# Another order of 1589 words for block-sparse attention and a token and channel mixer on one Trainium2 core

## The chip, the cores and the metric

The kernel runs on one core of one Trainium2 chip. The core has five engines that run side by side, each through its own instructions in a fixed order: TensorE (PE in the profile, with PEld for its weight loads), VectorE (DVE), ScalarE (ACT), GpSimd (POOL) and SyncE (SP). They meet at semaphores. Transfers are done by 16 DMA engines, which POOL, SP and ACT give work to. The metric is the device time of one execution in microseconds (us), lower is better. The time before is 292.2 us, the median of three runs (292.03 to 292.49).

## The reference

Attention over 4 batches, 8 heads, 768 positions and 64 features, with a mask in blocks of 32; then, on the 512 features of the joined heads, a mixer over tokens and one over channels.

```python
scores = scale * np.matmul(q, k.transpose(0, 1, 3, 2))
mask = np.abs(blk_i - blk_j) <= 1                   # neighbours
mask |= (blk_i == 0) | (blk_j == 0) | (blk_i == 23) | (blk_j == 23)
# ... and three sampled key blocks for each query block
scores = np.where(mask, scores, -1e9)
x = softmax(scores) @ v                             # heads side by side: [4, 768, 512]
a1 = alpha1 * x + beta1
u = x + lam * np.einsum('ts,bsd->btd', w_tok, a1)   # token mixer, 768 x 768
a2 = alpha2 * u + beta2
out = u + lam * (np.maximum(a2 @ w_ch1, 0.0) @ w_ch2)   # hidden layer of 2048
```

## The kernel before

**Words.** All work is cut into steps of a fraction of a microsecond up to a microsecond, and a step is called by a word: letters for the kind, a number for the piece, and after a colon a PSUM bank or the engine that copies (d: VectorE, a: ScalarE). A string named ORDER lists 1589 words. The kernel goes through it once and emits each word's instructions; a last pass ties the instructions of each engine to that order. Nothing else schedules. Two words on the same engine run in ORDER's order; words on different engines run as soon as the semaphores let them.

```python
    for word in ORDER.split():
        ...
        step[kind](int(n), *args)
    bank_order(tc, list(nc.cur_bb.bb.instructions), psum[:].tensor.name, 8)
    pin_order(nc, tc)
```

**Attention.** The 32 heads are 16 pairs. A pair's scores are cut into nine units of 1024 columns, numbered through: pair p has units 9p to 9p+8.

- lq, lk, lv load a pair's queries, keys and values (L437, issued by POOL, converted to 16 bits on the way, six buffers in turn). A load waits for its buffer and for the landing of the load eight before it. F and a tiny copy on POOL (L435) hold later loads back until DVE gets to F.
- cq, ck, cv put what was loaded into the layout that is needed (L419 on ACT, L421 on DVE).
- For the pairs 0 to 4, H transposes one head on PE (L355), and hq, hk copy queries and keys out of PSUM (L419, L421). The mask of blocks rides along as 24 more rows of queries and keys, so these matmuls have 88 rows. hm copies the 24 rows for the second head's query buffer (L587). For the pairs 5 to 15, tq and tk transpose by DMA, issued by SP (L593).
- q computes a unit's scores into two PSUM banks. q0 to q44 are matmuls of 88 rows (L624). From q45 on, a q word is four matmuls of 64 rows by 256 columns (L634), two of which run side by side in the halves of the array.
- e is the exp of a unit on ACT, 1024 columns from PSUM to SBUF (L645).
- m masks a unit of the pairs 5 to 15 on DVE by a minimum with a table (L655). The table is made once: M writes 24 rows (L532, DVE) from the mask rows in the fourth query buffer, which a transfer on SP (L401) fills ahead of ORDER; N spreads them to DRAM and O reads them back (L538 and L545, SP).
- p and r multiply by the values (L661), n and nt divide by the sums into x (L709, L712, L695, L696).

**Token mixer.** lt loads w_tok in three parts (L460), lt1 for W2 and W3, lt2 for W4 and W5, lt0 for W0 and W1. W transposes one block on PE (L496) and w copies it (DVE). lc loads alpha, beta and lam; L scales them (L506, L508). a and b make the mixer's input (L733, L739), k is 18 matmuls (L763), and x adds the result to x (L772).

**Channel mixer.** lw and lx load its weights (L479, L485), S, T, P and V prepare them. u casts x, U transposes it (on PE at L806 or by DMA at L800). The first batch's hidden layer is f, four matmuls of 384 columns into one bank (L828), emptied by g with bias and relu on ACT (L842) or DVE (L844); it is the stretch f0 to f31, and f32 to f63 are half of the next batch. Later hidden layers use fewer products: y is two matmuls (L997), d and D finish them (L1023, L1025, L866, L1033, L1035), after sums of weights and inputs by V and Y. The second layer is h, eight matmuls of 256 columns (L907), with sums A before and o after it on DVE (L866). s stores (L934). z is a filler matmul on zeros (L315), which keeps PE busy near the start.

**Banks.** PSUM has eight banks. A PE word that writes a bank waits until ACT or DVE has read what stood in it. A q word takes two banks; f, k, h, y, H and W take one.

The order at the start, before ORDER, is fixed: first loads, mask rows, the first head's transposes. The first q word starts at 5.83 us.

Of the kernel before, what the change touches and what calls it, by code (L numbers as in the profile page):

```python
# [72 lines left out]
m58 e59 p46 h17 m53 u8:a m47 u9:a q57:2 q55:3 F36 o2 e57 p47 U4 o14 p51:3 m59 h4 ck11:a m56 p52 e55
p53 nt15 lk14 q63:2 nt17 h18 e63 o3 q64:1 m57 q54:3 e64 q71:2 m60 h5 o15 e54 p57:2 a5 p58 h6 e71 b5
p59 ck12:a m64 q70:2 q62:3 nt19 e70 h19 lk10 m71 e62 q69:1 m54 q61:2 h20 F47 A5 ck9:a m55 p54:6
cq9:a k11:7 lv11 o16 e61 o4 tq9 lq13 h7:1 x11 cq10:a m62 k10:0 tk9 e69 m61 lv9 p60:7 A6 q67:2 tq10
m69 p55 e67 p56 o6 q80:1 x10 p61 e80 p62 nt18 q66:2 h8 nt20 e66 m70 q78:1 ck10:a q68:3 a6 p69:0 e68
p70 lk13 h9 m66 b6 e78 p71 o7 q65:2 q76:3 m63 u10:a q75:1 e65 nt23 h10 m67 u11:a p63:0 cv8:d k12:4
e76 m65 U5 lq12 m68 p66:5 e75 p64 x12 p67 tk10 p68 o8 q81:3 nt22 q86:1 e81 p65 h11 nt21 e86 m75
q74:2 q73:3 a7 e74 k13:0 b7 e73 q72:1 x13 q77:2 o9 u12:a k14:0 u13:a m76 e72 U6 k15:6 x14 A7 e77  # L80
p75:0 p76 x15 q79:1 u14:a m72 q85:2 u15:a h12 m77 e79 U7 m73 p77 e85 q82:3 m80 q93:1 s5 h13 m78 e93
tq11 m79 p78:4 p72:5 m74 e82 p73 p79 tk11 o10 p80 p74 q84:1 P1:d q87:3 nt24 e84 s0 f37:1 m86 tk12
f35:5 e87 nt26 f39:2 ck13:d g35:a m84 lq14 f54:3 g37:a nt25 g39:a q89:2 cv9:d q95:3 e89 q94:0 g54:d
lv10 f38:2 m82 e95 f32:3 P5:d P7:d f34:4 g32:a P6:d f48:5 e94 ck14:d m85 lk15 p84:3 a8 g34:a q83:3
q98:0 e83 p85 cq12:d f47:4 F44 F41 cv11:d tq12 lv15 m81 e98 p86 f61:6 g47:d lv12 g48:a p81:7 m83
q92:0 g61:a q88:2 b8 g38:a p82 f49:6 nt28 e92 m98 f36:2 e88 g49:d f63:3 m89 g36:a q106:0 m87 q91:2
g63:a p83 f51:6 e106 nt27 f56:2 m88 g51:a p87:3 cq13:d e91 f41:7 V0 m94 p88 g56:a q90:0 q96:2 cv10:d
g41:a m93 f52:2 e90 m92 p89 f57:6 m95 g52:a f53:7 e96 V2 p93:2 nt29 g57:a q97:0 q99:2 cq14:d e97
f33:3 m96 tq14 m91 p94 e99 p95 k16:6 m97 tk13 g33:a nt31 g53:a q104:0 m90 q102:1 s2 e104 q103:2 x16
f62:7 s1 a9 e102 tq13 p90:6 p91 p96:0 m99 p92 g62:a p97 nt30 tk14 p98 e103 f60:1 nt32 q113:1 m104  # L90
g60:a q100:2 s3 q105:3 e113 m102 s4 f59:0 b9 k17:1 e100 m113 F45 m103 lq15 e105 f55:2 x17 f44:3 lv14
g59:a m100 g55:a q108:2 m106 q107:0 lv13 e108 q101:3 m105 k18:2 a10 e107 p102:4 f50:5 m108 e101 x18
p99:0 p100 b10 g50:a f58:1 m101 g44:a p103 g58:a q131:3 m107 q115:1 p105:5 A20 e115 f45:1 A12 p106
e131 p104 A16 p101 p107 nt33 g45:a q112:1 k21:6 nt34 e112 nt35 q116:0 A21 q111:1 e116 q130:2 a11
# [5 lines left out]
p129:6 u19:a p130 m128 p131 e117 U9 k23:7 a12 e132 h40 o26 U10 nt43 cv15:a h41 x23 b12 u23:a q138:1  # L100
m127 q118:2 q119:3 e118 o34 h32 V5 cv13:a h21:0 m132 e119 m134 k25:4 o27 e138 k24:5 A14 x25 q142:1
o18 q143:3 A15 p126:4 p127 e143 x24 h33 m118 e142 p132:5 m117 h34 m138 p133 o28 p134 q141:1 nt44
q139:3 e141 p117:1 m143 p128 p118 h22 e139 nt42 m119 q135:1 a14 q125:2 e135 k22:6 b14 u24:a p119
e125 x22 h23 m141 u22:a q120:1 nt39 q140:2 e120 q137:3 U11 m142 k29:1 o19 e140 V1 k28:2 m125 u25:a
x29 e137 p141:3 U12 p142 m120 p143 h24 u29:a m139 m140 q123:2 q121:3 o20 e123 p138:1 x28 p139 h25
# [973 lines left out]
```

## Time and profile before

| | |
|---|---|
| median of three runs | 292.2 us (292.03 to 292.49) |
| the profiled execution | 291.82 us, of which the span from first to last instruction is 290.1 us |
| granted TensorE clock | 1.000 |
| exps on ACT, L645 | 145 instructions, 140.4 us |
| q matmuls, L634 and L624 | 396, 29.8 us, and 120, 25.8 us |
| h matmuls, L907 | 672, three groups of 35.8, 24.6 and 24.4 us |
| f matmuls, L828 | 256, 45.9 us |
| k matmuls, L763 | 576, 36.8 us |
| masks on DVE, L655 | 99, 61.2 us |
| moved by DMA | 30.95 MB, mean 107 GB/s |

The view of groups lists busy time per line, engine and operation. Busy time adds instructions that overlap on an engine once; a matmul's end is modelled, so the starts of matmuls are the surer numbers. A view of windows gives each engine's busy time in a stretch; a view of waits says which engine stood still before which line and what it waited for last; the chain is the series of steps that ended last; the timeline lists instructions in order, merging like ones. Idle time in square brackets stands ahead of an instruction.

### The profile page before, as it was taken

What the parts mean: (1) busy time and instruction counts of PE and PEld (TensorE: products, weight loads), DVE (VectorE), ACT (ScalarE), POOL (GpSimd) and SP (SyncE); (2) the same over time, 40 slices, a digit from 0 to 9 for tenths busy, and PEclk for the clock granted to TensorE, in tenths of its full rate; (3) what the DMA queues carried; (4) which work ended last, traced back from release to release, by engine and by line L of the source; (5) the groups of instructions that cost most, each with busy time, mean ns of one, the idle gap of its engine ahead of it and who ended that gap; (6) DMA issues with size and microseconds to landing.
All of it is one profiled execution on the core that took longest, in us unless ns stands there. A gap on an engine that the chain in (4) does not pass through costs nothing.

```text
span 290.1 us, 8529 instructions
## 1 busy us (share of the span) xinstructions
PE 283.9 (98%) x3538; PEld 213.6 (74%) x3538; DVE 263.8 (91%) x595; ACT 234.0 (81%) x350; POOL 53.3 (18%) x102
## 2 busy tenths in 40 slices
PE   8899999999999999999999999999999999999995
PEld 3677888755677878866677877888766788866884
DVE  5689997689999999999999999999999998699983
ACT  5999998849999999999999999968989860279500
POOL 8545734300621241024005000000000000000000
PEclk9999999999999999999999999999999999999999
DMA  6999999999983498499278002404110140330014
GB/s 161 189 246 210 195 211 194 203 165 176 168 115 30 53 140 118 74 164 135 27 186 146 7 2 57 85 3 47 37 75 0 19 112 0 148 145 1 2 42 177
DMA packets 47927, 30.95 MB, mean 107 GB/s; under 512 B 28792, under 2 KB 43984, under 8 KB 47888
## 3 DMA queue, kind: packets, MB, share of 16 engines
q0 software_dynamic: 15936, 15.21, 34.6%
q1 hardware_dynamic: 31340, 14.32, 24.3%
q10 hardware_dynamic: 612, 0.87, 0.8%
q8 instruction: 28, 0.46, 0.6%
q14 instruction: 11, 0.09, 0.1%
HBM read 31.16 MB, written 6.88 MB: 131 GB/s over the span
## 4 chain that ended last, share of the span: by engine, by line
PE 87%; ACT 5%; DMA 4%; DVE 2%; issue 1%; POOL 0%; ACTq 0%
PE psum L907 26%; PE psum L997 13%; PE psum L828 12%; PE psum L661 11%; PE psum L763 11%; PE psum L634 9%; PE psum L624 4%; DMA wtk<-in_moe_w_tok_dram 3%; ACT hts L842 2%; ACT eT L645 2%; DMA k2f<-in_k_dram 1%; PE psum L806 1%; PE psum L355 1%; DVE a1p L733 0%; ACT rel L419 0%
## 5 line engine op out<-in xcount | busy, mean ns | idle before, releaser
L645 ACT ACTIVATE eT<-psum 128x1024 f16<-128x1024 f32 (+1 forms) x145 | 140.4, 1028 | 9.3 <-PE psum L634 5.4
L655 DVE TENSOR_TENSOR eT<-eT,maskT 128x960 f16<-128x960 f16 x99 | 61.2, 650 | 0.0
L907 PEld LDWEIGHTS <-hts 128*128 128x128 bf16 x480 | 45.1, 98 | 8.5 <-issue 2.1
L661 PEld LDWEIGHTS <-eT 128*128 128x128 f16 x1152 | 44.4, 97 | 8.3 <-issue 1.7
L661 PE MATMUL psum<-vext,eT 128*128 128x65 f16 x1152 | 48.5, 193 | 0.0
L828 PE MATMUL psum<-uT,w1b 128*128 128x384 bf16 (+1 forms) x256 | 45.9, 327 | 0.1
L1023 ACT ACTIVATE snap<-psum,b1t 128x384 f32<-128x384 f32 x44 | 23.7, 581 | 17.7 <-PE psum L997 13.4
L763 PE MATMUL psum<-a1p,wtokT 128*128 128x128 bf16 x576 | 36.8, 219 | 0.2 <-DVE x_sb L772 0.2
L763 PEld LDWEIGHTS <-wtokT 128*128 128x128 bf16 x576 | 33.2, 98 | 4.1 <-DVE x_sb L772 0.8
L907 PE MATMUL psum<-w2t,hts 128*128 128x256 bf16 x288 | 35.8, 273 | 0.0
L866 DVE TENSOR_TENSOR x_sb<-x_sb,psum 128x256 f32<-128x256 f32 (+1 forms) x61 | 30.7, 514 | 4.7 <-PE psum L907 4.5
L828 PEld LDWEIGHTS <-w1b 128*128 128x128 bf16 x256 | 23.0, 98 | 16.1 <-ACT b1t L419 0.9
L842 ACT ACTIVATE hts<-psum,b1t 128x384 bf16<-128x384 f32 x53 | 29.2, 602 | 0.9 <-PE psum L828 0.5
L634 PE MATMUL psum<-qx,kx 64*128 64x256 bf16 x396 | 29.8, 272 | 0.0
L866 DVE TENSOR_TENSOR hts<-snap,psum 128x384 bf16<-128x384 f32 x48 | 24.7, 547 | 2.7 <-PE psum L997 2.3
L624 PE MATMUL psum<-qx,kx 88*128 88x512 bf16 (+1 forms) x120 | 25.8, 326 | 1.3 <-ACT eT L645 1.0
L907 PE MATMUL psum<-w2b,ss 128*128 128x256 bf16 x192 | 24.6, 273 | 0.0
L907 PE MATMUL psum<-w2b,hts 128*128 128x256 bf16 x192 | 24.4, 273 | 0.0
L634 PEld LDWEIGHTS <-kx 64*128 64x128 bf16 x396 | 15.2, 94 | 8.4 <-issue 3.5
L907 PEld LDWEIGHTS <-ss 128*128 128x128 bf16 x192 | 18.0, 98 | 3.8 <-issue 0.6
L772 DVE TENSOR_TENSOR x_sb<-x_sb,psum 128x384 f32<-128x384 f32 x32 | 17.4, 546 | 1.0 <-PE psum L763 0.8
L997 PEld LDWEIGHTS <-w1b 128*128 128x128 bf16 x128 | 12.1, 98 | 6.6 <-DVE hts L866 0.3
(103 smaller groups left out, 362.5 us busy)
## 6 DMA issues: line engine op xcount, KB each, us to landing
out_dram<-x_sb SPq DMA_DIRECT2D x17, 256.0 KB, 2.6
v<-in_v_dram POOLq DMA_DIRECT2D x16, 192.0 KB, 6.3
k<-in_k_dram POOLq DMA_DIRECT2D x15, 192.0 KB, 6.2
q<-in_q_dram POOLq DMA_DIRECT2D x15, 192.0 KB, 7.1
...
```

The lines of the kernel that those rows point to most:

```text
L624: nc.tensor.matmul(t[:, f : f + w], kx[h][0:KC, ts(jt, P)], qx[h][0:KC, c : c + w], start=True, stop=True,)
L634: nc.tensor.matmul(t[:, (2 * a + j) * TH : (2 * a + j + 1) * TH], kx[h][r, ts(2 * g + j, P)], qx[h][r, ts(th, TH)], start=True, stop=True,)
L645: nc.scalar.activation(eTs[n][:, c], t[:, c], AF.Exp, bias=EXPB, scale=SCALE)
L655: nc.vector.tensor_tensor(out=e, in0=e, in1=mask, op=ALU.min)
L661: nc.tensor.matmul(ops[key][:, t * VW : t * VW + D + 1], eTs[n][:, c : c + P], vext[n // NU % NV][:, a, jt, 0 : D + 1], start=(first and z ...
L763: nc.tensor.matmul(t[:, j, :], wtokT[:, s, ts(3 * g + j, P)], a1p[p][:, s, :], start=(s == 0), stop=(s == NT - 1),)
L828: nc.tensor.matmul(hps[i][:, 0:w], w1b[:, dk, ts(f, P)], uT[b][:, dk, hf * HS : hf * HS + w], start=(dk == 0), stop=(dk == 3),)
L842: nc.scalar.activation(hts[kk][:, f, :], t[:, 0:HS], AF.Relu, bias=b1t[:, f : f + 1], scale=1.0)
L866: nc.vector.tensor_tensor(out=out, in0=in0, in1=in1, op=op)
L907: nc.tensor.matmul(cps[b, q][:, side * HD : (side + 1) * HD], lhs[:, nk, :], rhs[:, nk, :], start=(z in (0, 6) and nk == 0), stop=(nk == H ...
L997: nc.tensor.matmul(chains[key], lhs[:, dk, ts(f, P)], rhs[:, dk, :], start=(z in (0, 1, 5) and dk == 0), stop=(dk == 1), skip_group_check= ...
L1023: nc.scalar.activation(dst, t, act, bias=bias, scale=1.0)
```

## The change

Only ORDER differs. Both strings have the same 1589 words if the part behind the colon is left aside: every load, matmul, exp, copy and store is done once in each. What differs is the order, the bank that a PE word uses, and in 58 words the engine. On ACT the casts cq4, cq5, cq7, cq15, cv5, cv7, cv8 and further u, g, d and D words come from DVE, and ck5, ck7, ck12, cv12 and others go to DVE; in sum cq on ACT goes from 3 to 7, ck from 8 to 5, cv from 4 to 6, g from 53 to 51 and D from 28 to 31. The words named in the change's title: M, which writes the rows of the mask's table, is called behind the 18th exp instead of the 41st; lq3 is the thirteenth load word instead of the eighth; tq6 keeps its place on SP, behind tq7 and ahead of tk8, tk7 and tq8, but the cast that it needs, cq6, moves from among the exps before the first hidden layer to near the end of that layer. The last words of ORDER, from h82 on, are the same in both.

The diff, cut to the stretches that the prediction speaks of:

```diff
--- before
+++ after
@@ the first 29 us @@
-lv0 lk1 lq1 q0:0 lt1 q3:1 cq0 e0 lq2 q2:2 H1:6 lk2 e2 hq1:d q1:0 lv1 z480:7 hm0 z480:7 e1 hk1:d
-cv0:d q5:2 ck1:d e3 lq3 q4:0 p0:6 lt0 e4 p1 p2 lt2 q6:1 cq1:d e5 p3 lk3 p4 H2:7 H3:0 lc2 e6 hk2:d
-q7:2 lc0 F35 W2:1 hq2:d e7 lc1 q8:1 hq3:d r4:7 lk4 r5 w2:d e8 q9:2 cq2:d r6 F24 ck2:d lv2 r7 e9 n0
-z480:1 q12:1 lq6 hk3:d r8 e12 q11:2 n1 W3:6 q10:0 e11 w3:d H5:7 cv1:d q16:1 hk5:d e10 lq4 H4:6 hk4:d
-W1:4 e16 q15:0 hq5:d p9:5 e15 p10 hq4:d q13:1 F21 cq3:d W0:7 F46 w1:d e13 lv4 q14:0 p11 W5:4 e14
-ck3:d q25:1 F22 w0:d lk5 p12 w5:d e25 p13 q19:3 n2 W4:4 e19 H6:0 F28 lx3 w4:d q22:1 hk6:d r13:1
-q17:2 e22 L1 q20:3 hq6:d e17 q24:1 L0 r14 H7:0 e20 q18:2 ck4:d a0 lv3 r15 e18 r16 r17 lc5 b0 q23:3
-e24 cv2:d k1:4 n3 lk6 e23 lx1 q21:1 cq4:d r22:1 F42 x1 H9:5 e21 lv6 q28:3 F38 a1 p18:4 lw0 e28 r23
+lv0 lq1 lk1 lt1 lk2 q0:0 q1:1 lq2 cq0 e0 q3:2 F22 hm0 lt2 H1:6 e3 lt0 hq1:d q2:0 lc0 z480:7 F24
+hk1:d e1 lv1 cv0:d q4:2 q6:3 e2 lc1 cq1:d q5:1 lc2 e4 p0:0 lq3 p1 ck1:d e6 lv2 q7:2 z480:1 lk3 p2
+e5 H2:1 q8:3 hk2:d e7 p3 p4 hq2:d H3:2 W2:3 e8 n0 q9:2 W3:1 hq3:d e9 r4:0 q10:3 F42 ck2:d r5 hk3:d
+lk4 r6 e10 q11:2 w3:d lw0 r7 F26 cq2:d r8 e11 w2:d q14:3 lv3 F23 n1 H5:1 e14 q13:1 lc5 hk5:d H4:4
+z480:0 e13 hk4:d q15:3 W4:0 hq4:d e15 W5:5 hq5:d q12:1 W0:4 w4:d e12 q17:3 w0:d q16:0 w5:d e17
+W1:4 cv1:d q23:1 w1:d lq4 p9:5 e16 p10 M0 r13:4 p11 lc4 L1 r14 e23 q18:3 F34 L0 lw1 p12 r15 e18 a0
+q26:0 r16 r17 e26 b0 q25:1 n3 q19:3 p13 q22:0 F21 e19 cq3:d F28 n2 k0:4 lk7 e22 ck3:d q20:3 lq8 x0
...
@@ M0 before @@
-u1:a M0 p36:0 v1:a F39 u5:d p37 p38 x6 q41:1 u6:d U0:1 e41 q43:2 u7:d U2:6 S6 p39 e43 U3:7 v0:d
...
@@ first hidden layer, f0 to f31 @@
-q44:1 v2:a v3:d p40 q42:2 F26 S7 r40:1 r41 e44 f0:6 f6:7 e42 f3:2 g0:a f5:3 cq5:d g3:d f1:6 tq5 lq11
-g5:a F31 n8 r42 f8:2 N0 r43 g8:d f17:0 tk5 f24:3 r44 g24:d f9:2 tk6 S1 f11:3 g9:a g1:d f15:4 ck7:a
-S4 f25:2 g11:a n9 f19:5 F30 S3 f12:1 S2 f2:3 g12:a S0 f31:6 g19:a S5 g15:a f26:1 T0 g2:a f10:4 f4:3
-g10:a T1 f28:5 g26:a f20:4 g31:a T2 g25:a f16:1 ck8:a f7:2 a4 g4:a f23:6 g17:a T3 O0 f13:3 g7:a tq7
-g28:a f18:0 cq8:d cv5:d g13:a f22:5 cv7:d tq6 g16:d g6:a f21:2 g23:d g22:a f27:1 g18:a tk8 P3:d
-g20:a g21:d f14:3 g27:a P2:d f29:2 tk7 g14:a F34 b4 lk11 f30:0 g29:d lk9 tq8 cq11:d q53:2 g30:a
+r42 e44 r43 cq8:d p37 S6 f9:3 lv5 cq5:a F27 S1 p38 q39:0 g9:a tq5 lq9 f0:4 e39 f5:3 N0 f6:6 g5:d
+f14:7 tk5 S4 f22:3 p39 tk6 p40 f7:0 n8 f11:1 g7:a F43 S0 r44 g11:a S3 f1:2 S5 f17:0 g1:a S2 f30:1
+g6:a T0 f16:2 g22:a f8:6 g17:a g14:d cq7:a f27:3 ck8:a f10:0 g27:d f3:7 F37 T1 g10:a f23:3 g0:a
+g3:d f15:0 T2 f13:4 g15:a f2:7 g16:a cv6:d f20:0 T3 g13:a f4:2 g2:a O0 n9 tq7 cv5:a f26:4 F38
+f12:7 a4 g26:a f19:5 g4:a b4 f18:4 F32 g12:d g19:a f21:2 F31 g8:a g30:d g20:d g23:a f29:5 cq6:a
+f28:1 g29:d cq9:a f25:0 tq6 F30 P2:d lq10 g18:d f24:3 g28:a P1:d g25:a lv8 f31:4 tk8 P3:d g21:a
+g24:d lk10 q51:0 g31:a h14:5 P4:d tk7 e51 lk11 A0 q49:1 q52:3 A8 lq13 e49 h0:4 tq8 A4 lk9 e52 o12
...
```

More of the change, by code (lines that the diff above doesn't have):

```diff
@@ L73 @@
[L73 to L94, printed above, removed]
@@ L100 @@
[L100 to L105, printed above, removed]
@@ new lines @@
+g24:d lk10 q51:0 g31:a h14:5 P4:d tk7 e51 lk11 A0 q49:1 q52:3 A8 lq13 e49 h0:4 tq8 A4 lk9 e52 o12
+q48:0 q50:1 A9 h15 e50 A1 o0 q47:3 P0:a A2 k8:2 A10 e47 h1 A5 e48 x8 h2 m49 A11 q45:0 q46:1 e45
+q53:3 m51 h16 tq9 m48 e53 p51:0 m52 k9:1 e46 o1 m53 p52 u8:a x9 q60:3 q58:1 m50 e60 p48:1 p49 m46
+p50 e58 h3 o13 F33 nt16 u9:a q59:3 m45 q57:1 e59 h17 A3 m47 e57 q56:3 p45:1 o14 p53 m58 e56 h18
+m57 ck10:a q54:1 o2 q55:3 nt17 h4 e54 lv9 o15 p57:0 e55 m59 p58 p46 o3 p47 cq10:a q61:1 m54 q63:3
+p59 e63 h5 lv7 nt15 nt19 e61 q70:3 a5 q68:0 h6 e70 b5 p54:2 m56 e68 k11:3 m55 ck9:a m61 q71:0
@@ new lines @@
+q62:3 m60 e71 p55 tk9 lq11 p56 x11 h19 e62 nt18 tq10 o4 q65:0 q66:1 e65 q75:3 m62 k10:4 U4 m70 e75
+m63 h7:0 ck11:a m71 tk10 p60:1 x10 h20 e66 lk13 A6 p61 cv8:a o6 q69:1 o16 q64:3 e69 h8 lk12 F45
+m65 m68 e64 p62 h9 nt20 cv7:a m69 q67:1 q78:2 m66 e67 q73:3 lq14 p69:1 m64 p70 p71 e73 p66:2 o7
+p63:3 m67 h10 e78 a6 p64 u11:a q76:3 nt23 q86:2 u10:a p65 b6 e86 p67 U5 p68 nt21 k13:1 e76 nt22 o8
+q80:1 x13 q72:2 q79:3 e72 A7 h11 a7 u13:a k12:1 e80 b7 m78 q85:2 e79 k15:2 x12 m80 u12:a k14:1 e85
+o9 U6 x15 q77:3 x14 q84:2 u15:a q74:1 m75 u14:a p78:1 h12 e77 m79 U7 m73 p79 e74 q82:3 m72 h13 m76
@@ new lines @@
+p89 f58:4 e90 nt29 f50:6 cv11:d a9 g56:a lv15 f37:5 g53:a m91 k16:7 g58:a g37:a m94 g50:a m90
+q102:0 q97:1 e102 q100:2 b9 k17:6 F46 cq12:d x16 e97 tq12 lk15 f39:0 e100 m97 p93:1 p94 p95 x17
+g39:a q106:1 m100 q98:2 e106 q105:3 tq14 k19:0 m92 e98 cv12:d m102 p90:2 tk13 f47:3 x19 e105 nt31
+p96:4 p91 g47:a s1 p97 m98 p92 u16:a f42:5 s0 m106 u17:a tq13 p98 nt30 g42:a q101:0 q107:3 nt32
+e101 q99:1 k18:5 tk14 V4 e99 a10 f63:4 s4 e107 m105 f59:0 s5 x18 s2 f32:1 g63:a m107 s3 g59:a
+f41:5 V0 g32:a q103:1 m99 g41:a q104:3 q111:0 e103 A20 p105:4 f33:5 b10 e111 p106 m103 p107 f35:2
@@ new lines @@
+A12 e104 k21:3 nt35 g33:a m104 g35:a q110:0 x21 q113:2 q112:3 m101 p102:2 e112 k20:3 A16 A21 e113
+p103 p104 x20 p99:6 e110 f43:7 nt34 A17 p100 g43:a p101 q108:0 m111 q109:1 f46:7 m110 e109 m113
+h35:4 e108 nt33 h28:5 o30 g46:a A22 q134:0 o24 q115:1 e134 q129:3 a11 h36 u21:a m109 f40:0 e129
+m108 h37 m134 e115 b11 p108:1 p109 u19:a m129 f44:6 u20:a A18 h29 g40:a m115 cq15:a f45:0 V2
+ck15:a p110 o31 h30 V5 u18:a tk15 g45:a nt36 h38 g44:a o25 U10 m112 q116:0 q130:1 A23 e116 q114:3
+h31 o32 tq15 e114 m116 p111:0 p112 o26 k23:1 cv14:a U9 m114 cv13:a V1 p113 p114:6 nt37 p115 e130
@@ new lines @@
+p116 h39 nt38 x23 q131:1 q118:3 o33 e131 q126:0 h32 a12 s11 e118 U8 h40 m130 e126 o27 q133:1
+q139:3 A19 e133 h41 m131 h33 e139 m126 o34 q128:0 q127:1 b12 e128 q117:3 A13 h34 m133 u23:a p129:4
+e117 o28 p130 p131 h21:0 nt43 e127 m118 q132:2 q119:3 m127 e132 q138:1 k22:1 m139 e138 m132 p126:4
+k25:5 m128 e119 x22 p127 o18 u22:a q120:1 x25 q140:3 e120 U11 p132:1 m117 p128 h22 A14 e140 A15
+p133 p134 cv15:a m119 q141:1 q125:3 e141 m138 k24:5 nt44 e125 h23 nt42 x24 p138:1 o19 q124:1
+q123:2 a14 e124 q142:3 p139 h24 Y8 e123 m140 p117:2 p118 o20 u24:a p119 b14 p140 e142 h25 nt39
```

78 lines of the change are left out of this document (40 added, 38 removed).

## The prediction

> **What bounds the kernel now.** I read the page first, then busy time by stage, then the list of PE's own waits, then the chain and the timelines at the places these named.
>
> ```profile
> span 290.1 us, 8529 instructions
> ...
> PE 283.9 (98%) x3538; PEld 213.6 (74%) x3538; DVE 263.8 (91%) x595; ACT 234.0 (81%) x350; POOL 53.3 (18%) x102
> ...
> PE 87%; ACT 5%; DMA 4%; DVE 2%; issue 1%; POOL 0%; ACTq 0%
> ```
>
> PE is busy for 98% of the span and carries 87% of the chain. No word is added or dropped, so the same matmuls run. The change can win only time in which PE stands still and what PE pays for the order itself; it can lose wherever a reordered word comes too late. The stages show where PE stands still now:
>
> ```profile
> core 0: us, PE busy (x) PEld busy (x) DVE busy (x) ACT busy (x) POOL busy (x), PEclk, DMA share, GB/s
> ...
> 5.80:12.00 6.20, 5.38 (x67) 3.56 (x68) 3.75 (x10) 5.47 (x7) 4.19 (x8) 1.00 1.13 175
> 12.00:20.00 8.00, 7.62 (x104) 5.45 (x102) 6.99 (x18) 7.89 (x9) 4.10 (x7) 1.00 1.20 208
> 20.00:29.00 9.00, 8.82 (x134) 6.53 (x132) 8.41 (x22) 8.91 (x11) 4.59 (x7) 1.00 1.23 238
> 29.00:50.00 21.00, 21.00 (x368) 17.88 (x365) 18.82 (x54) 20.22 (x24) 11.03 (x20) 1.00 1.16 200
> ...
> 62.00:76.00 14.00, 13.89 (x86) 7.55 (x85) 13.27 (x24) 12.06 (x32) 1.00 (x2) 1.00 1.21 186
> ...
> 120.00:206.00 86.00, 86.00 (x1265) 65.68 (x1261) 84.29 (x184) 79.80 (x109) 8.67 (x15) 1.00 0.46 77
> 206.00:286.90 80.90, 80.90 (x719) 61.85 (x716) 73.14 (x158) 46.44 (x95) 0.00 (x0) 1.00 0.18 62
> ```
>
> From 5.8 to 29 us PE lacks 0.82 + 0.38 + 0.18 = 1.38 us, and ACT is busy 7.89 of 8.00 and 8.91 of 9.00: there the exps on ScalarE set the pace. After 120 us PE has no gap at all. PE's waits by name:
>
> ```profile
> PE psum L624 <- ACT eT L645: 1.0, 2, 0.8
> ...
> PE psum L496 <- DMA wtk<-in_moe_w_tok_dram: 0.4, 2, 0.2
> ...
> PE psum L763 <- DVE x_sb L772: 0.2, 1, 0.2
> ```
>
> So the ground to be won lies in the first 29 us, a little in the first hidden layer (62 to 76 us), and in one token-mixing step.
>
> **The changes of array shape.** From pair 5 on, a q word is four matmuls of 64 rows (L634), and all other words use 128 rows.
>
> ```profile
> 87.61 0.54 PE psum L634 x8
> 88.15 0.98 PE psum L907 x8
> 89.13 0.49 PE psum L661 x16
> 89.62 0.87 PE psum L907 x8
> ...
> 94.30 0.76 PE psum L634 x12
> ```
>
> Twelve q matmuls take 0.76 and eight 0.54, so four cost 0.22 and a run has 0.10 on top. The h word ahead of a q run takes 0.98 where another takes 0.87: 0.11 more. A run of q words thus pays 0.21 us, however long it is. Counted in the two orders, the 99 such words stand in 46 runs before and in 44 after: 2 x 0.21 = **-0.4 us**. No wait is involved, so nothing can hide or undo it.
>
> **The first 29 us: the second head's keys.** DVE copies the second head's queries (hq1), then the mask rows (hm0, L587), then the keys (hk1), and PE's next q word needs the keys.
>
> ```profile
> 7.81 0.55 DVE L421 COPY qx<-psum 64x768 bf16<-64x768 bf16 x1 [0.81 <-PE psum L355]
> 8.38 0.35 DVE L587 COPY qx<-qx 24x768 bf16<-24x768 bf16 x1
> 8.74 0.56 DVE L421 COPY kx<-psum 64x768 bf16<-64x768 bf16 x1
> ...
> 9.40 1.02 PE L624 MATMUL psum<-qx,kx 88*128 88x256 bf16 x5 [0.79 <-ACT eT L645]
> ```
>
> The wait at 9.40 is named after ACT, but the keys were finished at 9.30. After, hm0 stands ahead of hq1 and fits into DVE's 0.81 us of idleness; hk1 follows hq1 at once. PE goes on at about 9.05: -0.35 us.
>
> **The first 29 us: the mixing weights.** W words transpose wtk, which arrives in three loads.
>
> ```profile
> 5.28 0.57 POOL L460 DMA_DIRECT2D wtk<-in_moe_w_tok_dram  x1
> ...
> 10.70 1.11 POOL L460 DMA_DIRECT2D wtk<-in_moe_w_tok_dram  x2
> ...
> DMA to landing us min/median/max: 8.0/8.3/9.5
> ```
>
> ```profile
> 12.47 0.60 PE L624 MATMUL psum<-qx,kx 88*128 88x512 bf16 x2
> 13.28 0.54 PE L496 MATMUL psum<-identb,wtk 128*128 128x128 bf16 x6 [0.22 <-DMA wtk<-in_moe_w_tok_dram]
> ...
> 18.45 0.50 PE L355 MATMUL psum<-identb,rel 128*128 128x128 bf16 x6
> 19.10 0.51 PE L496 MATMUL psum<-identb,wtk 128*128 128x128 bf16 x6 [0.15 <-DMA wtk<-in_moe_w_tok_dram]
> ...
> 23.07 0.60 PE L624 MATMUL psum<-qx,kx 88*128 88x512 bf16 x2
> 23.50 0.50 PE L496 MATMUL psum<-identb,wtk 128*128 128x128 bf16 x6
> 23.84 0.50 PE L355 MATMUL psum<-identb,rel 128*128 128x128 bf16 x6
> ```
>
> Undisturbed, a q word takes 0.43 (23.07 to 23.50) and a W or H word 0.34 (23.50 to 23.84). So W2 at 13.28 lost 13.28 - 12.47 - 0.43 = 0.38, and W1 at 19.10 lost 19.10 - 18.45 - 0.34 = 0.31. (The view shows less, 0.22 and 0.15, because a matmul's modelled end hides some 0.16 of each wait.) Both started as their load landed: 5.28 + 8.0 = 13.28. After, lt1 is still the fourth load and lands at 13.3 again. Ahead of W2 now stand, from 9.05 on, five q words (2.15), five p (0.245 each, from the 0.49 for 16: 1.2), two H (0.7) and a filler (0.2): 13.3, no wait to speak of. lt2 moves from tenth to seventh in the load queue, and lt0 from ninth to eighth with the same bytes ahead of it, so it lands at about 19.0 as before; but the words that use it, W0 and W1, now stand behind W4 and W5, which use lt2. From W2 to W4 PE has six q (2.6), four W or H (1.4), four and a half r (1.1) and a filler (0.2): 18.6; W0 comes 1.1 us later, 0.7 after its load. Both waits go: -0.7 us. The cover is thin for W2; without it 0.38 comes back.
>
> The page "DMA: Bandwidth & Descriptors" of the Trainium skill, section "Anatomy of one DMA", gives 2.0 us plus bytes over 436 GB/s for one such load. By that, wtk's 384 KB would land within 3 us of its issue, no W word would ever have waited, and the sum would lack these 0.7 us. The trace's 8.0 to 9.5 us says that a load waits behind those queued ahead; the trace decides.
>
> **What ScalarE lets through.** An exp follows the last one after 0.92 us when it is fed:
>
> ```profile
> 21.07 0.82 ACT eT L645
> ...
> 21.99 0.92 ACT eT L645
> ```
>
> Before the hidden layer there are 45 exps: 41 us that no order shortens. The 0.35 and 0.7 us reach the end only because each of those PE waits also left ScalarE unfed behind it. For the first 29 us I take the full 0.35 + 0.7 = **-1.0 us**; the ends are 0 (ScalarE takes it all back) and -2.5 (all of the 1.38 plus 0.16 for each of seven waits).
>
> **The first hidden layer.**
>
> ```profile
> 58.34 1.30 PE psum L828 x8
> ...
> 60.75 15.29 PE L828 MATMUL psum<-uT,w1b 128*128 128x385 bf16 x90
> 75.98 0.61 PE L634 MATMUL psum<-qx,kx 64*128 64x256 bf16 x8
> ...
> 68.91 0.72 ACT rel L419
> ```
>
> Eight matmuls take 1.30, so 90 need 14.6; they took 15.2 (60.75 to 75.98). The 0.6 us are waits for a bank that ScalarE had not yet read, where a head's cast (0.72) stands between two evacuations. After, ScalarE has six such casts in this block (cq5, cq7, ck8, cv5, cq6, cq9) instead of two (ck7, ck8), and two evacuations fewer (21 for 23; DVE has 11 instead of 9). Of the six, cq6 and cq9 come at the end, ahead of g28 and g25, whose banks are next wanted by k9 and p51, many words on. The other four stand ahead of g9, g10 (cq7 and ck8 both) and g26; behind f10 and f26 two other f words (1.3 us) come before their banks are taken again. ACT had 14.00 - 12.06 = 1.94 us free in the stretch. I take half the loss as gone, **-0.3 us**; the ends are -0.6 (all gone) and +2.3 (a rival, below).
>
> **Edits at nothing.** The mixing step that waited 0.2 for x (L772) has a like neighbour after: 0, ends -0.2 and +0.2. M0 (L532, the mask rows in the same shape as hm0's 0.35) moves from behind the 41st exp to behind the 18th, ahead of L1, L0, a0 and b0 on DVE, which k0 on PE waits for. DVE has 9.00 - 8.41 = 0.59 us free in that stage, so it finds room; without it M0 costs 0.35. M0's input, the mask rows of the fourth query buffer, is written by a transfer ahead of all the loads. N0 and O0 keep their places on SP between the same transposes. The transposes tq6, tk8, tk7 and tq8 issue later, since cq6 stands behind f29:
>
> ```profile
> DMA to landing us min/median/max: 2.7/2.8/11.4
> ```
>
> With this block ending near 74.3 (75.98 less the 1.7 of the sum), f29 three f words earlier puts tq6 near 72. q60, its first user, stands some 10.7 us of PE work behind q51, at 85: even the slowest landing, 11.4, is in time. lq3, called "sooner", is in fact the thirteenth load instead of the eighth; between wtk's last load at 19 and its cast, behind the 22nd exp (0.92 us each, so past 25), it has 6 us to land. From 120 us on PE has no gap and none that I find after: 0.
>
> **The sum.** -0.4 - 1.0 - 0.3 = -1.7 us. The profiled execution took 291.8 us (span 290.1), 0.4 under the median of 292.2. So 290.1 for such an execution, and **290.5 us** for the median.
>
> **Rivals.** *ScalarE takes the early gain back* (for: ACT is busy 8.91 of 9.00 there; against: it was unfed behind each PE wait). Left are the shapes and part of the hidden layer, -0.4 to -0.7: 291.5 to 291.8. Chance 0.16, half of it within what can be told.
>
> *The casts on ScalarE make the hidden layer slower.* A cast holds the evacuations behind it for 0.72, and PE, whose banks they free; two casts lost 0.6 before. If the four that count cost PE their whole time, 4 x 0.72 = 2.9, that is 2.3 more than now; with -1.4 from the other terms +0.9: 293.1. It turns the change into a loss from 0.5 a cast on (4 x 0.5 = 0.6 + 1.4). For: the two before already cost 0.3 each. Against: the free 1.94 us, and the f words between. Chance 0.14.
>
> *The change doesn't do what it says*: so it is for lq3, and it costs nothing either way.
>
> **How the numbers follow.** A measurement of this kernel can tell about 0.2%, 0.6 us, from no change. The forecast has 0.70; with -0.4 to -1.8 early and 0 to -0.6 in the hidden layer it reaches from -0.8 to -2.8, 291.4 to 289.4. With half of the first rival it makes 0.78 faster; 0.08 same; 0.14 slower. The range 289.4 to 292.5 adds the first rival and the milder part of the second; left out are deeper gains and the rest of the second, together under 0.2.
>
> **What would show it.** Right: the next q word after hk1 near 9.05; no wait for wtk; PE short of less than 0.7 us between 5.8 and 29; 90 hidden-layer matmuls in 14.6 to 15.0; 44 runs of L634. Wrong: waits for eT as long as before, L828 waiting for hts behind the casts, or any PE gap after 120 us.

## The result: 289.8 us after 292.2

The changed kernel takes 289.76 us (median of five runs, 289.27 to 289.83), the kernel before 292.20 (292.03 to 292.49). The ratio is 0.9905, with a 95% interval of 0.9882 to 0.9929. The profiled execution of after took 289.79 us with a span of 288.1, against 291.82 and 290.1. The forecast was 290.5, so the sign and most of the size were right. The experiments below show that two of its steps gave nearly the right number for a wrong reason, so that part of the agreement is luck.

The line numbers of after, and of the runs e5, e8, e11 and e12, are two higher than before: the wide q words are L626, the 64-row ones L636, the exps L647, f L830, h L909, W L498. The page of the profile after, engines and chain:

```profile
span 288.1 us, 8507 instructions
...
PE 283.5 (98%) x3538; PEld 214.4 (74%) x3538; DVE 263.9 (92%) x592; ACT 235.1 (82%) x353; POOL 54.0 (19%) x102
...
PE 97%; ACT 1%; DVE 0%; issue 0%
```

PE's busy time has hardly moved (283.9 to 283.5), but its share of the chain went from 87% to 97%. Before, the chain passed through ScalarE for 5% and through transfers for 4%, 8.3 us of that through one load of wtk; after, no transfer is left in it and 1% of ScalarE. These shares are not time in which PE stood still: the whole 8.3 us count, though the word behind that load waited only 0.3. By stage (columns as in the prediction):

```profile
5.80:12.00 6.20, 5.62 (x47) 3.10 (x46) 3.68 (x12) 5.40 (x8) 4.40 (x8) 1.00 1.18 192
12.00:20.00 8.00, 8.00 (x125) 6.34 (x124) 6.62 (x18) 8.00 (x10) 3.58 (x6) 1.00 1.14 221
20.00:29.00 9.00, 9.00 (x142) 6.83 (x140) 8.73 (x23) 8.78 (x10) 5.27 (x10) 1.00 1.21 216
29.00:50.00 21.00, 21.00 (x349) 17.47 (x348) 19.20 (x51) 20.57 (x25) 9.92 (x16) 1.00 1.20 207
62.00:76.00 14.00, 14.00 (x92) 8.32 (x92) 13.46 (x31) 13.11 (x29) 3.03 (x7) 1.00 0.63 119
```

Up to 29 us PE now lacks 0.58 us instead of 1.38, all of it before 12 us. In the first hidden layer it lacks nothing. The waits behind a q or a W word that the list of PE's waits still names:

```profile
PE psum L626 <- ACT eT L647: 0.3, 1, 0.3
```

The waits for wtk and for x are gone from the list, although the loads of wtk take no less time:

```profile
wtk<-in_moe_w_tok_dram POOLq DMA_DIRECT2D x3, 384.0 KB, 9.2
```

**Where the 2.0 us between the two profiled executions lie.** A view's idle time hides part of each wait, because a matmul's end is modelled. So I lay PE's words out without any wait, each with the spacing that such words keep in the trace of before where nothing stops them (wide q 0.436 us, 64-row q 0.223, k 1.005, f 0.65, h 0.872, y 0.324, H, W and U 0.34, p 0.245, and 0.19 for each run of 64-row words). The lost time at a word is its start in the trace, counted from the first q word, less its place in that layout, counted likewise. The rows of the table are places in the layout in us, numbered so that the first q word stands at 5.83:

```
place    before   after
 16       1.68     1.66
 20       2.10     1.73
 30       2.71     1.78
 62       3.12     2.03
 76       3.63     2.08
120       4.39     2.53
end       4.96     3.11
```

To 30 us after lost 0.93 less, from 30 to 62 us 0.16 less, in the hidden layer 0.46, from 76 to 120 us 0.31, and from there on the same. Two runs of 64-row words fewer give 0.38. That is 2.24 us; 0.20 is missing because the first q word itself started later:

```profile
5.83 1.40 PE L624 MATMUL psum<-qx,kx 88*128 88x512 bf16 x8 [0.34 <-ACT qx L394]
```

```profile
6.03 1.15 PE L626 MATMUL psum<-qx,kx 88*128 88x512 bf16 x4
```

This start is a matter of the execution and not of the order: in the fourteen profiles of this study it lies between 5.83 and 6.03, for both orders.

### The profile page after: what moved, and what is told of

Same layout as the page of the kernel before. It is cut to its first block, busy times and chain, and to the rows that moved or that the text cites. A ratio compares the mean times of both kernels' runs of the same rounds, so it can differ in the third digit from the quotient of the medians.

```text
span 288.1 us, 8507 instructions
## 1 busy us (share of the span) xinstructions
PE 283.5 (98%) x3538; PEld 214.4 (74%) x3538; DVE 263.9 (92%) x592; ACT 235.1 (82%) x353; POOL 54.0 (19%) x102
## 4 chain that ended last, share of the span: by engine, by line
PE 97%; ACT 1%; DVE 0%; issue 0%
PE psum L909 26%; PE psum L830 15%; PE psum L999 13%; PE psum L663 13%; PE psum L765 12%; PE psum L636 9%; PE psum L626 7%; PE psum L317 2%; ACT eT L647 1%; PE psum L357 1%; PE psum L498 1%; PE psum L808 0%; DVE x_sb L868 0%
## 5 line engine op out<-in xcount | busy, mean ns | idle before, releaser
L647 ACT ACTIVATE eT<-psum 128x1024 f16<-128x1024 f32 (+1 forms) x145 | 138.4, 1029 | 7.6 <-PE psum L636 5.7
L909 PEld LDWEIGHTS <-hts 128*128 128x128 bf16 x480 | 45.0, 98 | 8.3 <-issue 1.9
L663 PEld LDWEIGHTS <-eT 128*128 128x128 f16 x1152 | 43.5, 97 | 8.2 <-issue 1.7
L663 PE MATMUL psum<-vext,eT 128*128 128x65 f16 x1152 | 47.5, 193 | 0.1
L830 PE MATMUL psum<-uT,w1b 128*128 128x384 bf16 (+1 forms) x256 | 45.8, 326 | 0.0
L868 DVE TENSOR_TENSOR x_sb<-x_sb,psum 128x256 f32<-128x256 f32 (+1 forms) x61 | 31.3, 516 | 5.5 <-PE psum L909 5.1
L909 PE MATMUL psum<-w2t,hts 128*128 128x256 bf16 x288 | 35.1, 273 | 0.0
L830 PEld LDWEIGHTS <-w1b 128*128 128x128 bf16 x256 | 23.5, 98 | 14.6 <-issue 0.8
L1025 ACT ACTIVATE snap<-psum,b1t 128x384 f32<-128x384 f32 x43 | 22.9, 585 | 8.7 <-PE psum L999 8.6
L636 PE MATMUL psum<-qx,kx 64*128 64x256 bf16 x396 | 29.4, 271 | 0.0
L844 ACT ACTIVATE hts<-psum,b1t 128x384 bf16<-128x384 f32 x51 | 27.7, 596 | 0.4
L626 PE MATMUL psum<-qx,kx 88*128 88x512 bf16 (+1 forms) x120 | 26.0, 330 | 0.5 <-ACT eT L647 0.3
L909 PE MATMUL psum<-w2b,ss 128*128 128x256 bf16 x192 | 24.4, 273 | 0.0
L909 PE MATMUL psum<-w2b,hts 128*128 128x256 bf16 x192 | 24.0, 273 | 0.0
L636 PEld LDWEIGHTS <-kx 64*128 64x128 bf16 x396 | 15.5, 94 | 8.9 <-ACT eT L647 2.4
L909 PEld LDWEIGHTS <-ss 128*128 128x128 bf16 x192 | 17.9, 98 | 3.5 <-DVE x_sb L868 0.6
```

What stands on the lines that cost most here:

```text
L626: nc.tensor.matmul(t[:, f : f + w], kx[h][0:KC, ts(jt, P)], qx[h][0:KC, c : c + w], start=True, stop=True,)
L636: nc.tensor.matmul(t[:, (2 * a + j) * TH : (2 * a + j + 1) * TH], kx[h][r, ts(2 * g + j, P)], qx[h][r, ts(th, TH)], start=True, stop=True,)
L647: nc.scalar.activation(eTs[n][:, c], t[:, c], AF.Exp, bias=EXPB, scale=SCALE)
L663: nc.tensor.matmul(ops[key][:, t * VW : t * VW + D + 1], eTs[n][:, c : c + P], vext[n // NU % NV][:, a, jt, 0 : D + 1], start=(first and z ...
L830: nc.tensor.matmul(hps[i][:, 0:w], w1b[:, dk, ts(f, P)], uT[b][:, dk, hf * HS : hf * HS + w], start=(dk == 0), stop=(dk == 3),)
L844: nc.scalar.activation(hts[kk][:, f, :], t[:, 0:HS], AF.Relu, bias=b1t[:, f : f + 1], scale=1.0)
```

## The experiments

### The two waits of the first 29 us, taken away in the kernel before

e1, the second head's keys sooner:

```diff
-lk2 e2 hq1:d q1:0 lv1 z480:7 hm0 z480:7 e1 hk1:d
+lk2 e2 hm0 hq1:d q1:0 lv1 z480:7 z480:7 e1 hk1:d
```

> The kernel before, with hm0 alone moved ahead of hq1. Theory (the prediction's step on the second head's keys): hk1 ends 0.35 us sooner and PE goes on at 9.05 instead of 9.40; but W2 still waits for its load, which lands at 13.28 whatever PE does, so W2's wait of 0.38 grows to about 0.7 and next to nothing is left at 20 us: 0.0 to -0.1 us at the end. Rival 1: the 0.35 us reach the end, 291.85. Rival 2 (exps set the pace): PE does not go on sooner at all, the word at 9.40 was waiting for the exp it is named after; 0, and the wait at 9.40 is unchanged.

e2, the mixing weights' words one q word later:

```diff
-q7:2 lc0 F35 W2:1 hq2:d e7 lc1 q8:1 hq3:d
+q7:2 lc0 F35 hq2:d e7 lc1 q8:1 W2:1 hq3:d
...
-W1:4 e16 q15:0 hq5:d
+e16 q15:0 W1:4 hq5:d
```

> The kernel before, with W2 and W1 each moved one q word later, so that wtk has landed when PE gets there. Theory (the prediction's step on the mixing weights): both waits for wtk vanish from the list of PE's waits, PE has 0.7 us less idleness by 20 us and keeps it to the end: 291.5. Rival (ScalarE takes it back): the waits for wtk vanish, but PE waits for exps instead, by the time of 29 us PE stands where it stood, 0.0 to -0.2 us at the end.

e3, both:

> The kernel before with both edits, hm0 ahead of hq1 and W2 and W1 one q word later. Theory: the two together give the -1.0 us of the prediction's first stage, 291.2, the 0.35 of hm0 being kept now that W2 has room. Rival (ScalarE takes it back): 0 to -0.3 us, with more waits for eT in the list instead.

Measured: 292.05, 292.17 and 292.07 us, before, taken beside them, 292.31; the ratios are 0.9991 (0.9966 to 1.0017), 1.0001 (0.9979 to 1.0024) and 0.9991 (0.9965 to 1.0016). None of the three is told from no change. The intervals are wide, up to 0.75 us either way: the times alone exclude neither the 0.35 of e1 nor the 1.0 of e3, and the 0.7 of e2 only just, so the traces have to decide. The lost time by place:

```
place    before   e1     e2     e3     e4*
 10       1.08    0.62   0.93   0.82   0.93
 20       2.10    1.68   2.56   2.41   2.54
 30       2.71    2.28   3.49   3.14   3.14
* e4 (below) has the order of before up to the hidden layer
```

e1 did bring PE on sooner, by 0.3 to 0.45 us at 10 us. But e4, which has the order of before here, lost 0.43 more than before by 30 us: executions of one order differ by that much, so e1's 2.28 is no sure gain. In e2 the exchange is plain in the list of PE's waits:

```profile
PE psum L624 <- ACT eT L645: 1.3, 3, 0.8
PE psum L496 <- DMA wtk<-in_moe_w_tok_dram: 0.3, 1, 0.3
```

W2 no longer waits; the q word now ahead of it does, for an exp (it lost 0.47 us, W2 in before 0.37). W1 still waits, since its load landed near 20 us this time. In e3 neither W word waited noticeably, and yet 3.14 us were lost by 30: H2 waited for a cast instead (0.7 us).

### One load moved, so that W1 need not wait

e9 moves lt0 ahead of lq3 in the kernel before:

```diff
-cv0:d q5:2 ck1:d e3 lq3 q4:0 p0:6 lt0 e4
+cv0:d q5:2 ck1:d e3 lt0 lq3 q4:0 p0:6 e4
```

> The kernel before with one load moved: lt0, the third of wtk that W1 and W0 use, ahead of lq3. In the profiles of the order before, lq3's issue stood 2.0 us on GpSimd's queue until cv0 had freed its buffer, and lt0 behind it was issued at 10.6; now it is issued near 8.0, and, the loads moving some 200 KB per us, it lands about 1 us sooner. W1 waited 0.3 to 1.0 us for it in the five profiles with this order. Theory 2 (up to 28 us the exps of ScalarE leave no slack, so that a wait which is gone is gained in full): W1's wait vanishes, PE has lost 2.2 to 2.5 us at 30 us instead of 2.7 to 3.1, -0.5 us, 291.7. Rival (ScalarE takes it back): the wait vanishes, and the loss at 30 us stays 2.7 to 3.1; 292.2.

Measured: 292.00 us, ratio 1.0002 (0.9984 to 1.0019). GpSimd's timeline of before and then of e9 show that the move did what it should:

```profile
9.99 0.72 POOL L437 DMA_DIRECT2D q<-in_q_dram  x1 [2.01 <-DVE vext L421]
```

```profile
7.94 0.61 POOL L460 DMA_DIRECT2D wtk<-in_moe_w_tok_dram  x1
10.00 0.72 POOL L437 DMA_DIRECT2D q<-in_q_dram  x1 [1.45 <-DVE vext L421]
```

lq3 needs a buffer that cv0 frees, and while it waits all loads behind it on the queue wait too; lt0 is now issued at 7.94 instead of behind it. PE's timeline of e9 around W1:

```profile
18.62 0.50 PE L355 MATMUL psum<-identb,rel 128*128 128x128 bf16 x6
18.95 0.50 PE L496 MATMUL psum<-identb,wtk 128*128 128x128 bf16 x6
19.46 0.61 PE L624 MATMUL psum<-qx,kx 88*128 88x512 bf16 x3
...
20.83 0.50 PE L496 MATMUL psum<-identb,wtk 128*128 128x128 bf16 x6
21.29 0.61 PE L624 MATMUL psum<-qx,kx 88*128 88x256 bf16 x3
```

W1 starts 0.33 behind the H word: no wait. But the q words behind W1 and W0 come 0.51 and 0.46 after them instead of 0.34: 0.17 and 0.12 went to exps. From place 16 to place 30 e9 lost 0.93 us. The four profiles with the order of before there (before, e4, e6, e7) lost 1.03, 1.68, 1.02 and 1.52, and W1 waited 0.32, 0.98, 0.30 and 0.82 in them. Less W1's wait each of the four lost 0.70 to 0.72, and e9 0.93. So 0.2 of W1's wait is free, since the exps take it anyway, and what goes beyond that is lost one for one. Both readings have a part of it; by the median the edit is worth nothing that can be told, within half a microsecond either way. (W2 waited 0.63 in e9, for its own load, but at 16 us e9 stood as before did, at 1.73 for 1.68.)

### The whole early part at once

e5 takes the first 229 words from after, and all other words in the order of before.

> The first 229 words of the order after (to about 40.5 us, M0's and lq3's new places among them), then all other words in the order of before. Theory 2, formed from the first four runs (in the first 30 us no single wait decides; the exps of ScalarE stand one behind another, and what counts is how much other PE work lies between the q words, which only the whole new order changes): PE has lost some 1.8 us at 30 us instead of 2.3 to 3.5, and all later losses of before (0.3 at 50 us, 0.2 each at f10 and f22, 0.2 at k14) come back as they were: about 291.3, 0.9 less than before. Rival (the early part of the profile of after was a lucky execution, in which its loads landed soon): 292.0 to 292.3, with a wait for wtk in the list.

Measured: 309.22 us, ratio 1.0583 (1.0568 to 1.0598). The seam spoiled the time: near 41 us ScalarE met the cast cq6, which the order of before has early, while its load lq6 came only behind the seam, because the order of after has it late. ScalarE stood 15 us; hk8 stood behind it and PE's r31 behind hk8.

```profile
56.79 0.83 ACT L421 COPY rel<-q 128x768 bf16<-128x768 bf16 x1 [15.09 <-DMA q<-in_q_dram]
```

Up to the seam it is a clean test, and there it answers: 2.25 us lost at 30 us. The order after lost 1.78 in its own profile, 2.10 in e8 and 1.91 in e12 (both below; e12 has hm0 moved); the mean of the four is 2.0. The order of before lost 2.71, 3.14, 3.09 and 3.11 (before, e4, e6, e7), mean 3.0, and 2.28 to 3.49 with edits in this stretch. So the early part is worth 1.0 us by the traces, and the two groups of four do not overlap. No run's total time shows it by itself.

### The early edits taken back in the kernel after

e12 puts hm0 behind hq1 again; e11 puts lq3 ahead of lt2 again.

```diff
-q3:2 F22 hm0 lt2 H1:6 e3 lt0 hq1:d q2:0
+q3:2 F22 lt2 H1:6 e3 lt0 hq1:d hm0 q2:0
```

> The kernel after with hm0 moved back behind hq1, so that hk1 has it ahead again. The prediction's step: hk1 comes 0.35 us later, and the end with it: 290.1. Theory 2: PE's word behind hk1 starts 0.3 later, but the wait at q7 (11.55), where PE meets the exps again, becomes shorter by as much; from 12 us on all is as it was: 0 to +0.1, 289.8.

```diff
-q3:2 F22 hm0 lt2 H1:6 e3 lt0 hq1:d
+q3:2 F22 hm0 lq3 lt2 H1:6 e3 lt0 hq1:d
...
-e4 p0:0 lq3 p1 ck1:d
+e4 p0:0 p1 ck1:d
```

> The kernel after with lq3 moved back from the thirteenth load to the seventh among all, ahead of lt2 and lt0 (as before, where it also came ahead of both). 192 KB more stand ahead of the two loads of wtk, so they land about 1 us later. Theory 2: W4 (19.3 us) or W0 (20.4 us) waits for wtk, by 0.3 to 1.0 us; after 18 us the exps of this order have slack, but the wait is PE's own, and it stays to the end: +0.3 to +1.0, 290.1 to 290.8. Rival (the place of lq3 is nothing that PE sees, since W4 and W0 stand late enough): no wait for wtk, 289.8.

Measured: e12 289.59 us, e11 290.25, with ratios to before of 0.9912 (0.9893 to 0.9931) and 0.9932 (0.9916 to 0.9948). e12 keeps all of the gain. PE's timelines, of e12 and then of after:

```profile
9.63 1.26 PE L626 MATMUL psum<-qx,kx 88*128 88x512 bf16 x7 [0.51 <-DVE kx L423]
...
11.48 0.60 PE L626 MATMUL psum<-qx,kx 88*128 88x512 bf16 x2
```

```profile
8.94 1.70 PE L626 MATMUL psum<-qx,kx 88*128 88x512 bf16 x8
...
11.69 0.61 PE L626 MATMUL psum<-qx,kx 88*128 88x512 bf16 x2 [0.26 <-ACT eT L647]
```

In e12 PE waits for the keys at 9.63, and then not for the exp at q7; in after it is the other way round, and afterwards e12 is no later: at 16 us it had lost 1.50, after 1.66. From q1, the second q word, to q7 both lost the same 1.25 us.

e11 is slower. It was taken beside e12: the spans of its six executions are 288.3 to 288.8 us, those of e12's six 287.6 to 288.2 and those of after's five 287.6 to 288.1. By the medians lq3's earlier place costs 0.4 to 0.6 us. GpSimd's timeline of e11 shows that lt0, with one more load ahead of it, was held until an earlier load had landed; in after it was issued by 8.4:

```profile
9.91 0.55 POOL L462 DMA_DIRECT2D wtk<-in_moe_w_tok_dram  x1 [1.36 <-DMA v<-in_v_dram]
```

W0, which uses this load, then lost 0.31 us at 20.5. But e8, which has lq3 where after has it, lost 0.28 at the same word, and the profiled executions of e11 and e12 differ by only 0.1 us. So the cost is measured, and the word that pays for it stays open.

### The hidden layer

e4 takes one of the two casts off ScalarE:

```diff
-f15:4 ck7:a S4
+f15:4 ck7:d S4
```

> The kernel before with one cast of the first hidden layer, ck7, moved from ScalarE to VectorE. Theory (the prediction's step on the hidden layer): the stall at f10, behind that cast, vanishes, the one at f22, behind ck8, stays: -0.3 us, 291.9, half of the 0.6 us that the layer loses. Rival 1 (not the casts but the row of evacuations on ScalarE without one on VectorE makes the stall): f10's stall shrinks by what ScalarE gains but comes back a few words later, 0 to -0.1. Rival 2: VectorE, with 0.73 us free in the 14 us and 0.56 more to do, becomes late: 0 to +0.3.

Measured: 292.52 us, ratio 1.0011 (0.9984 to 1.0038), so no change that can be told. f10 lost 0.20 us as before and f22 0.22. f12 lost 0.27, where before lost next to nothing, waiting for n9 on VectorE, behind the added cast. The timeline of before's ScalarE, and then of e4's weight loads and ScalarE, shows both that wait and why f10 gained nothing:

```profile
63.90 0.16 ACT L419 COPY b1t<-psum 128x1 f32<-128x1 f32 x1 [1.15 <-PE psum L828]
64.09 1.05 ACT L842 ACTIVATE hts<-psum,b1t 128x384 bf16<-128x384 f32 x2
65.03 0.16 ACT L419 COPY b1t<-psum 128x1 f32<-128x1 f32 x1
65.22 0.58 ACT L842 ACTIVATE hts<-psum,b1t 128x384 bf16<-128x384 f32 x1
```

```profile
64.03 2.40 PEld L828 LDWEIGHTS <-w1b 128*128 128x128 bf16 x16 [0.49 <-DVE x_sb L712]
64.90 0.16 ACT L419 COPY b1t<-psum 128x1 f32<-128x1 f32 x1 [2.11 <-PE psum L828]
```

Without the cast ScalarE merely stood still longer, 2.11 us instead of 1.15, for f12. Behind g12 stood g19 and g15, and g15 (65.03 to 65.80) empties the bank that f10 needs. Its f word had long been done. So e7 moves words within ScalarE's own order, with no work added or taken away:

```diff
-f12:1 S2 f2:3 g12:a S0 f31:6 g19:a S5 g15:a
+f12:1 S2 f2:3 g15:a g12:a S0 f31:6 g19:a S5
...
-f16:1 ck8:a f7:2 a4 g4:a f23:6 g17:a T3 O0 f13:3 g7:a tq7 g28:a
+f16:1 f7:2 a4 g4:a f23:6 g17:a T3 O0 f13:3 g7:a tq7 g28:a ck8:a
```

> The kernel before with two words of ScalarE moved in the first hidden layer: the evacuation g15 ahead of g12 (into the 1.15 us in which ScalarE stood idle for f12) and the cast ck8 behind g28. ScalarE has the same work as before. Theory 3, formed since ck7 on VectorE left f10's stall as it was (0.20): f10 waits because g15, which frees its bank, stands behind g12, for whose f word ScalarE was idle; f22 waits because g28 stands behind the cast ck8. So both stalls (0.20 and 0.22) vanish: -0.4 us, 291.9. Rival (ScalarE as a whole is too late in this stretch): each stall comes back at the next word whose bank is late, 0 to -0.1.

Measured: 291.48 us, before 292.09, ratio 0.9979 (0.9967 to 0.9991): a gain, of 0.6 by the medians. By the trace the lost time from 62 to 76 us fell from 0.51 to 0.05, as much as in after. PE's timeline of e7, and then of after:

```profile
60.16 15.85 PE L828 MATMUL psum<-uT,w1b 128*128 128x385 bf16 x96
75.95 0.61 PE L634 MATMUL psum<-qx,kx 64*128 64x256 bf16 x8
```

```profile
58.90 15.79 PE L830 MATMUL psum<-uT,w1b 128*128 128x385 bf16 x96
74.63 0.39 PE L636 MATMUL psum<-qx,kx 64*128 64x256 bf16 x4
```

96 matmuls in 15.79 and 15.73 us are 0.164 each; before it was 15.23 for 90, 0.169 each.

### The shapes and the later part

e8 splits nine runs of 64-row q words in the kernel after, at places like this one:

```diff
-q70:3 a5 q68:0 h6 e70
+q70:3 h6 a5 q68:0 e70
```

> The kernel after with nine runs of 64-row q words split: one word (seven h, two k) is moved ahead of the last q word of the run that stood before it, so that the 99 words stand in 53 runs instead of 44. Theory (the prediction's step on array shapes): each run costs 0.10 in the run and 0.11 in the word ahead of it, so 9 x 0.21 = +1.9 us, 291.7 where after takes 289.8. Rival 1 (only the 0.10 is real): +0.9, 290.7. Rival 2 (the price was of the stalls at those places, not of the shape): 289.8.

Measured: 292.28 us, 2.5 more than after (before, taken beside each of them, was 292.09 and 292.20). One of the nine places in the timeline, after and then e8:

```profile
95.33 0.61 PE L636 MATMUL psum<-qx,kx 64*128 64x256 bf16 x8
95.87 1.05 PE L909 MATMUL psum<-w2b,hts 128*128 128x256 bf16 x8
96.75 0.41 PE L663 MATMUL psum<-vext,eT 128*128 128x65 f16 x8
```

```profile
95.95 0.39 PE L636 MATMUL psum<-qx,kx 64*128 64x256 bf16 x4
96.27 1.05 PE L909 MATMUL psum<-w2b,hts 128*128 128x256 bf16 x8
97.25 0.39 PE L636 MATMUL psum<-qx,kx 64*128 64x256 bf16 x4
97.57 0.42 PE L663 MATMUL psum<-vext,eT 128*128 128x65 f16 x8
```

The same three words, two q and one h, take 1.42 and 1.62 us up to the start of the p word: 0.20 for one run more. Over the whole kernel nine times 0.19 is 1.7. The rest are three new waits of moved words, 0.27, 0.13 and 0.28 (q58, p114, q140), and 0.3 of the first 30 us. The price is real, and the two runs that the change saves give 0.4.

e6 has the first 418 words from before, and then the order of after.

> The first 418 words of the order before (to about 75 us), then all other words in the order of after. Theory: this half holds the two q runs saved (-0.4) and the mixing steps, where the trace of after lost 0.3 us less: about 291.5, 0.7 less than before; the two stalls at f10 and f22 stay. Rival 1 (a run of 64-row words costs nothing that the count of runs shows): only the 0.3, 291.9. Rival 2 (the gain of this half needs what the first half brings, since PE that runs sooner meets other waits): 292.2.

Measured: 299.06 us, ratio 1.0244 (1.0221 to 1.0268). Here too the seam spoiled the time: PE waited 3.5 us for one exp just behind it.

```profile
PE psum L634 <- ACT eT L645: 4.0, 2, 3.5
```

Behind the seam, from 80 to 120 us, it lost 0.41 us, where before lost 0.75 and after 0.41. So the mixing steps' gain belongs to the later words alone. The total can't tell whether it and the 0.4 arrive at the end.

### All single edits together

e10 has e9's, e1's and e7's edits in the kernel before.

> The kernel before with four words moved: lt0 ahead of lq3, hm0 ahead of hq1, g15 ahead of g12, and ck8 behind g28. By the prediction's steps: 0.35 for the keys, 0.3 to 1.0 for W1, 0.42 for the two stalls of the hidden layer: -1.3 us, 290.9. Theory 2: hm0 brings PE on sooner at 9 us, but the exps, one behind another, take most of that back by the next q words: -0.1 instead of -0.35, so -1.0 us, 291.2. In both, 0.9 us of what the whole change brings stays out: the two q runs, the mixing steps, and the slack that its first 30 us have.

Measured: 291.37 us, ratio 0.9977 (0.9963 to 0.9992), the same as e7 alone. At 20 us it had lost only 1.64, better than after; at 30 us 2.64, like the others of its order. W4 and q24 lost 0.36 and 0.35 in between. A head start in this stretch did not last. No edit tried here makes an order faster than after.

## Why the prediction was right, and where it was not

**The signs named beforehand all came.** The q word behind hk1 started at 8.94, no word waited for wtk, PE lacked 0.58 us up to 29, 90 hidden-layer matmuls take 14.8 at the pace of after, and there are 44 runs of L634. They could not tell whether each term of the sum was right: the start at 8.94 came, and was worth nothing.

**Array shapes, -0.4: right.** e8 measured 0.20 at a place of its own; the terms 0.10 and 0.11 stand.

**The keys, -0.35: the step failed, its value is 0.** The prediction took PE's earlier start behind hk1 as gained. The start did come sooner in e1, and came later again in e12, but q words a little further on wait for the same row of exps. It named the danger itself ("the 0.35 and 0.7 us reach the end only because each of those PE waits also left ScalarE unfed behind it"); for the keys that was not so, since in after ScalarE was busy for all of the 8.00 us from 12 to 20 us.

**The mixing weights, -0.7: right that the waits go, wrong that their sum is what comes.** Moving W2 gave a wait for an exp in its stead (e2). W1's wait was not 0.31 but anything from 0.30 to 0.98 in profiles of the same order, and 0.2 of it cost nothing (e9).

**The stage's -1.0: the right number, by luck.** Measured are 0.93 in the two executions and 1.0 between the means of four profiles each, though neither of the two terms that it was added up from is worth its size. What carries it is the order as a whole. The first rival, that ScalarE takes the gain back, held by the medians for every early edit in the kernel before, also for several together (e3, e10), and fails for the whole order. Of the single moves in this stretch only lq3's shows in a time: taken back in the kernel after it costs 0.4 to 0.6 (e11). For the rest I can offer a reason, which was counted and not tested by itself: between the places 22 and 30 us the order before has nine wide q words (the 20th to the 28th) and after has seven (the 21st to the 27th). An exp follows the last one after 0.92 us (the prediction's rows). Nine need 8.3 us of ScalarE beside 8.0 us of PE, so any wait there, whatever its cause, is lost for good; seven need 6.4, and ScalarE catches up. Before lost 0.5 to 0.6 us there beside W1's wait. Its timeline shows the edge:

```profile
25.94 0.61 PE L624 MATMUL psum<-qx,kx 88*128 88x512 bf16 x3 [0.18 <-ACT eT L645]
```

This q24 lost 0.34 us, and 0.34 or 0.35 in each of the eight other profiles that begin with this order; in after no q word of the stretch loses anything.

**The hidden layer, -0.3: mis-sized, and its cause half wrong.** It measured -0.46. The prediction blamed the casts. One stall (f22) goes when the cast ck8 stands behind g28. The other (f10) has nothing to do with a cast: an evacuation whose f word was done stood behind one whose f word was not (e4 and e7). So the second rival, by which four casts would turn the change into a loss from 0.5 each on, rested on a price of 0.3 for each of the two casts before: one of them, ck8, cost 0.22 where it stood, the other nothing. After has six casts there and lost 0.05.

**Edits at nothing.** From 30 to 62 us 0.16 and from 76 to 120 us 0.31 came as well, which the prediction put at 0 and had within its 0.2 only for one x. Before lost 0.11 at q56, 0.21 at k14 and the rest in small pieces; after 0.07 at q75. N0, O0 and the later transposes cost nothing that the trace shows. From 120 us on the two lost 0.57 and 0.58, as forecast.

lq3's later place is not nothing, as the prediction had it: it takes bytes and a held issue out of the way of wtk's loads, and e11 measures 0.4 to 0.6 us for it.

M0 is not quite nothing either. The prediction found room for it on VectorE. There M0, L1, L0, a0, b0 and n3 run one behind another, and k0 starts when n3 has read its bank. In after this came almost in time, and k0 lost 0.04 us; in e8, with the same words up to there, M0 took 0.50 us instead of 0.41, and k0 lost 0.19. In e5, e11 and e12 L1 waited for the load of beta, by 0.44, 0.29 and 0.36 us, and k0 lost 0.64, 0.34 and 0.34. VectorE's timeline of e12, and then PE's:

```profile
22.70 0.35 DVE L534 TENSOR_SCALAR maskT<-qx 24x768 f16<-24x768 bf16 x1
23.41 0.69 DVE L508 TENSOR_TENSOR b_bcb<-lb 128x512 bf16<-128x512 f32 x1 [0.36 <-DMA lb<-in_moe_beta_dram]
...
26.44 0.56 DVE L714 TENSOR_TENSOR x_sb<-psum,rcp 128x384 f32<-128x384 f32 x1
```

```profile
27.06 1.12 PE L765 MATMUL psum<-a1p,wtokT 128*128 128x128 bf16 x17 [0.17 <-DVE flag L456]
```

So the profiled execution of after was a fortunate one at this word, and its 1.78 us at 30 the least of all profiles.

**The rule for one load.** By the page "DMA: Bandwidth & Descriptors" of the Trainium skill, section "Anatomy of one DMA", no word would have waited for wtk. The traces disagreed before the change and after it: 8.3 and 9.2 us at the median from issue to landing, as the rows have it. That the single edits found these waits worth next to nothing does not bear the rule out, since the waits were there.
